# Pooled attention and a gated feed-forward on one core: query loads moved to later slots of a hand-written plan

## The chip, the core and the metric

The kernel runs on one core of a Trainium2 chip. The metric is the device time in microseconds (us) of one execution. TensorE (PE, with its weight loads PEld), VectorE (DVE), ScalarE (ACT) and GpSimd (POOL) work side by side, each in its own program order, and wait for each other by semaphores. SyncE (SP) issues all DMAs here, in its program order too; an issue that has to wait holds up all issues behind it.

## The reference

```python
# q, k, v: (8, 8, 576, 64)  (batch, head, token, dim), float32; pool = 8, so 72 pooled keys
k_p = k.reshape(B, H, 72, 8, 64).mean(axis=3)
v_p = v.reshape(B, H, 72, 8, 64).mean(axis=3)
scores = (1 / sqrt(64)) * q @ k_p.T
attn = softmax(scores)                     # with 1e-09 added to the sum
x = (attn @ v_p) -> (4608 tokens, 512)     # token-major, heads side by side
out = ((x @ w1) * (x @ w2)) @ w3 @ w_out   # w1, w2: 512x1024; w3: 1024x1024; w_out: 1024x512
```

## The kernel before

The product w3 @ w_out is computed once, at the start, into `W`; after that, chunk by chunk of 384 tokens (12 chunks, `NCH`), `a = x @ w1`, `b = x @ w2`, their product g and `out = g @ W`. Float32 factors are split in a high and a low part (fp32r), and each product is done in three passes (high-high, high-low, low-high).

The order of the work is written out by hand. Each step is entered with `at(kind, k, step, ...)` in a plan at a time k, and the plan is then sorted by the whole slot k // 1, the kind ("L" for loads, "P" for the work of VectorE, ScalarE and GpSimd, "M" for the large products, "A" for the products of attention), the fraction of k, and the order of entry. The steps are emitted in that order, so a slot is no time on the chip; it sets the order in which each engine finds its instructions. In a slot, steps of the same fraction stand in the order in which they were entered: first the feed-forward, then attention with its query steps, then keys and values.

A chunk m has 24 slots, three for each of 8 column blocks j:

- slot 3j: `a_mm` (12 matmuls into the PSUM bank `a`), then at 3j + 1 `a_post` (ScalarE, L573) copies it out;
- slot 3j + 1: `b_mm` (12 matmuls, L563, into the bank `b`); at 3j + 2 `b_post` multiplies it on VectorE (L583), which empties the bank, and ScalarE casts the high part gh (L584); at 3j + 2.5 `g_lo` makes the low part gl on VectorE (L589);
- slot 3j + 5: `out_mm` (9 matmuls, L598) with gh and gl. The banks `a` and `b` have one buffer each.

In the slots of chunk m, the attention of chunk n = m + 1 is worked out. A chunk's 384 tokens lie in one batch (three tiles of 128 tokens) or, for n = 1, 4, 7, 10, in two (four tiles of 96). For tile t, counted from the first slot of chunk m:

- scores `s_mm` (TensorE, L404) at slots -1 + 3t and 3t, `soft1`, `soft2`, `soft3` (the softmax on VectorE and ScalarE; `soft3` also gathers the remainder columns R, L451 and L453);
- `pt_turn` at 4 + 3t: VectorE transposes 32x32 blocks of the probabilities and of R into the tile T, which has one buffer (L487, twice);
- `pt_move` at 5 + 3t: SyncE issues a DMA for every 32 tokens (four or three) that move the blocks of T into PTx (L503);
- `pt_split` at 7.5 + 3t: ScalarE casts the high part PTh (L152), VectorE subtracts for the low part (L153);
- `av_mm` (TensorE, L537 to L540) from slot 16 (three tiles) or 18 (four tiles), and `av_post`, which makes the next x.

The queries come in with `load_q`, one call for each of four head pairs, as 32-element rows (4 DMAs a call for a chunk in one batch, 8 for one in two batches; L265), and `tr_q` turns them on VectorE (L276). For chunk n >= 2 the loads stand 18 to 15 slots ahead of the first slot k of chunk n - 1, so at slots 6, 7, 8, 9 of chunk n - 2, and the turns at slots 15 to 18 of it. The buffers `qs` and `qT` have one copy each.

Keys and values of a batch: `load_k` in slots 8, 10, 12, 14 of the chunk before, `prep_k` on GpSimd (a tree of three additions, L362 to L364). For batches from 2 on, `load_v` stands at slots 1 and 2 of the chunk in whose slots the batch is first attended to, `load_vr` (the remainder values: 8 DMAs, L356) at 3, `prep_v` (GpSimd) at 6 and 7, `prep_v2` (a ScalarE cast, L374, then GpSimd, L375) at 9 and 10, `prep_vr` (the GpSimd tree, then three ScalarE operations, L381 to L384) at 10, and `prep_vr2` (GpSimd, L392) at 11. Such chunks are m = 2, 3, 5, 6, 8, 9. The staging tiles `st` of keys, values and remainder values share four buffers in turn.

The outputs of chunk m - 1 are copied out and stored in slot 3 (`out_post`, L610 to L613).

Of the kernel before, what the change touches and what calls it, by code (L numbers as in the profile page):

```python
# [18 lines left out]
def kernel(  # L19
# [228 lines left out]
    def tok_tiles(n):  # L248
        res = []
        for (b, s0, cnt, off) in pieces(n):  # L250
            step = 128 if cnt == 384 else 96
            for x in range(0, cnt, step):
                res.append((b, off + x, step))
        return res
# [382 lines left out]
    def at(kind, k, fn, *args):  # L637


        plan.append((k // 1, "LPMA".index(kind), k % 1, len(plan), fn, args))  # L640

    def plan_att(n, s_at, ds, pt_at, av_at):


        for t in range(len(tok_tiles(n))):
            for half in range(2):
                k = s_at[t] + ds * half
                at("A", k, s_mm, n, t, half)
                at("P", k + 1, soft1, n, t, half)
            at("P", k + 2, soft2, n, t)  # L650
            at("P", k + 3, soft3, n, t)
            if n > 1:
                at("P", k + 4, pt_turn, n, t)
                at("L", k + 5, pt_move, n, t)
                at("P", pt_at[t], pt_split, n, t)
                continue
            k = pt_at[t]
            at("A", k, pt_mm, n, t)
            at("A", k, ptr_mm, n, t)
            at("P", k + 1, pt_post, n, t)  # L660
            at("P", k + 1, ptr_post, n, t)
        for pr in range(NPR):
            at("A", av_at[pr], av_mm, n, pr)
            at("P", av_at[pr] + 1, av_post, n, pr)

    def plan_k(b, k, load, prep, d):
        for pr in range(NPR):
            at("L", load + 2 * pr, load_k, b, pr)
            at("P", prep + d * pr, prep_k, b, pr)
        at("A", k, kt_mm, b)  # L670
        at("P", k + 1, kt_post, b)

    def plan_v(b, load, load_r, prep, prep2, prep_r):
        for hf in range(2):
            at("L", load + hf, load_v, b, hf)
            at("P", prep + hf, prep_v, b, hf)
            at("P", prep2 + hf, prep_v2, b, hf)
        at("L", load_r, load_vr, b)
        at("P", prep_r, prep_vr, b)
        at("P", prep_r + 1, prep_vr2, b)  # L680

    def plan_q(n, load, d_load, turn, d_turn):
        for pr in range(NPR):
            at("L", load + d_load * pr, load_q, n, (pr,))
            at("P", turn + d_turn * pr, tr_q, n, pr)

    def plan_q3(n, load, turn):
        for pr in range(NPR):
            at("L", load[pr], load_q3, n, pr)
            at("A", turn[pr], q3_turn, n, pr)  # L690
            at("P", turn[pr] // 1 + 1.2, q3_post, n, pr)
# [10 lines left out]
    for s in range(NS):  # L702
        k = F0 + 2 * s
# [19 lines left out]
    for j in range(NJ):  # L723
        for w in range(2):
            i = 2 * j + w
            at("L", K0 + 8.5 + i, load_w12, j, w)
            k = M0 - 6 + 1.25 * i
# [5 lines left out]
    for m in range(NCH):  # L733
        m0 = M0 + 3 * NJ * m
        for j in range(NJ):
            k = m0 + 3 * j
# [9 lines left out]
    for n in range(1, NCH):  # L746
        k = M0 + 3 * NJ * (n - 1)
        nt = len(tok_tiles(n))
        s0, pt, av = (3, 5.5, 20.5) if n == 1 else (-1, 8.5, 18) if nt == 4 else (-1, 8.5, 16)
        s_at = [k + s0 + 3 * t for t in range(nt)]  # L750
        plan_att(n, s_at, 1, [x + pt for x in s_at], [k + av + pr for pr in range(NPR)])
        if n == 1:
            plan_q3(n, [K0 + 8.5 + 1.5 * pr for pr in range(NPR)], [K0 + 12, K0 + 13, K0 + 15, K0 + 15.5])
        else:
            plan_q(n, k - 18, 1, k - 9, 1)
    for b in range(1, B):
        k = M0 + 3 * NJ * (3 * (b // 2) + b % 2 - 1)
        if b == 1:
            plan_k(b, k + 3.5, k - 7, k - 4, 2)
            plan_v(b, k + 5, k + 6.5, k + 7, k + 16, k + 13)  # L760
        else:
            plan_k(b, k - 3, k - 16, k - 13, 2)
            plan_v(b, k + 1, k + 3, k + 6, k + 9, k + 10)

    for _, _, _, _, fn, args in sorted(plan, key=lambda x: x[:4]):
        fn(*args)
# [30 lines left out]
```

## Time and profile before

| | |
|---|---|
| median of 3 runs | 830.6 us (828.93 to 830.96) |
| the profiled execution | 824.39 us |
| its span, first to last instruction | 822.6 us |
| mean granted TensorE clock | 0.979 of full speed |
| busy share: PE, DVE, ACT, POOL | 94%, 57%, 34%, 24% |
| DMA issues: q (L265), PTx blocks (L503), remainder values (L356) | 208, 120, 64 |

A row of the timeline has the start, the duration, the engine, the line, the operation with what it writes and reads, and in brackets how long the engine had been idle before it and what ended that. "SPq" is SyncE's queue: a row there is the stretch in which so many DMAs were issued. The table of stretches gives start and end, the length, the busy time of each engine with its instructions, the granted clock, the share of DMA engines busy and GB/s. In the table of waits stand the total, the number and the longest.

### The profile page before, as it was taken

To read this page: it belongs to the slowest core of one execution; us is meant where nothing else is said; L and a number is where in the kernel's file an instruction comes from. 1 tells how busy PE (TensorE), PEld (TensorE's weight loads), DVE (VectorE), ACT (ScalarE), POOL (GpSimd) and SP (SyncE) were. 2 spreads that over 40 slices of the span, in tenths; PEclk is the share of its full clock that TensorE was granted. 3 is DMA by queue.
4 is the path that set the end of the run, shared out by engine and by line. 5 is a ranking of instruction groups with operands and counts; after the bars stand their busy time and mean duration, and the time that the engine had idled before them with its cause. 6 is when DMAs were issued, how large, how long until landed. Compare 5 with 4: busy or idle time off the path is not lost.

```text
span 822.6 us, 11446 instructions
## 1 busy us (share of the span) xinstructions
PE 769.5 (94%) x4146; PEld 712.4 (87%) x4146; DVE 470.3 (57%) x939; ACT 280.1 (34%) x694; POOL 196.6 (24%) x234
## 2 busy tenths in 40 slices
PE   8889877999998998999998998999998999999997
PEld 7668866999987997999987988999987988999997
DVE  7868899384563474484563565474554565572112
ACT  5577654232332332232332322232332232332211
POOL 2335556007027002007037011007036011000000
PEclk9999999999999999999999998999999998999999
DMA  9998940047146040055146140065146140020101
GB/s 326 280 206 219 268 110 1 1 109 162 39 82 143 34 91 16 5 129 137 40 88 142 40 82 15 14 126 131 47 82 141 39 83 15 27 70 0 39 1 39
DMA packets 123913, 74.43 MB, mean 90 GB/s; under 512 B 75600, under 2 KB 107600, under 8 KB 123856
## 3 DMA queue, kind: packets, MB, share of 16 engines
q1 hardware_dynamic: 123856, 73.69, 37.0%
q8 instruction: 33, 0.54, 0.3%
q14 instruction: 24, 0.20, 0.1%
HBM read 52.43 MB, written 9.44 MB: 75 GB/s over the span
## 4 chain that ended last, share of the span: by engine, by line
PE 64%; DVE 15%; DMA 8%; SPq 4%; ACT 4%; issue 3%; POOL 2%; DVEq 0%; ACTq 0%; POOLq 0%
PE b L563 20%; PE o L598 18%; PE a L563 17%; DVE T L487 2%; PE att L404 2%; SPq L265 2%; DMA st<-in_k_dram 2%; SPq L503 2%; DMA PTx<-T 2%; DMA qs<-in_q_dram 2%; DVE mx L420 1%; DVE E L422 1%; ACT E L425 1%; DMA raw<-in_moe_w_dram 1%; DVE E L442 1%
## 5 line engine op out<-in xcount | busy, mean ns | idle before, releaser
L563 PE MATMUL b<-xT,hl 128*128 128x384 f32 x1152 | 229.7, 349 | 26.6 <-DVE a L583 26.1
L563 PEld LDWEIGHTS b<-xT,hl 128*128 128x128 f32 x1152 | 206.1, 194 | 29.8 <-DVE a L583 28.9
L563 PE MATMUL a<-xT,hl 128*128 128x384 f32 x1152 | 223.4, 342 | 0.0
L563 PEld LDWEIGHTS a<-xT,hl 128*128 128x128 f32 x1152 | 203.9, 190 | 4.5 <-POOL hl L153 0.2
L598 PE MATMUL o<-Wc,gh 128*128 128x512 f32 x576 | 182.8, 399 | 0.0
L362 POOL TENSOR_TENSOR st<-st 72x512 f32<-72x512 f32 (+1 forms) x53 | 72.2, 1362 | 218.9 <-DMA st<-in_k_dram 205.3
L598 PEld LDWEIGHTS o<-Wc,gh 128*128 128x128 f32 x576 | 108.9, 192 | 17.5
L598 PE MATMUL o<-Wc,gl 128*128 128x512 f32 x288 | 114.7, 398 | 0.0
L583 DVE TENSOR_TENSOR a<-b,a 128x384 f32<-128x384 f32 x96 | 53.0, 552 | 103.2 <-PE b L563 103.2
L584 ACT CAST gh<-a 128x384 fp32r<-128x384 f32 x96 | 49.3, 513 | 160.0 <-DVE a L583 160.0
L573 ACT COPY a<-a 128x384 f32<-128x384 f32 x96 | 45.9, 479 | 114.6 <-PE a L563 92.4
L425 ACT ACTIVATE E<-E 128x288 f32<-128x288 f32 (+1 forms) x70 | 31.2, 445 | 123.1 <-DVE E L422 123.1
L589 DVE TENSOR_TENSOR gl<-a,gh 128x384 fp32r<-128x384 f32 x96 | 59.9, 624 | 22.7 <-ACT gh L584 22.3
L598 PEld LDWEIGHTS o<-Wc,gl 128*128 128x128 f32 x288 | 54.8, 190 | 12.9
L375 POOL TENSOR_TENSOR vbd<-vm,vbd 64x256 fp32r<-64x256 f32 x16 | 11.9, 745 | 223.3 <-ACT vbd L374 223.1
L153 DVE TENSOR_TENSOR PTx<-PTx,PTh 128x512 fp32r<-128x512 f32 (+1 forms) x33 | 22.2, 673 | 72.0 <-ACT PTh L152 71.6
L549 DVE TENSOR_TENSOR xT<-att,xT 128x384 fp32r<-128x384 f32 x48 | 26.5, 556 | 60.9 <-ACT xT L548 60.9
L404 PE MATMUL att<-kbd,qT 128*128 128x144 f32 (+1 forms) x320 | 52.2, 286 | 0.5 <-ACT E L430 0.5
L426 DVE TENSOR_REDUCE sm<-E 128x4 f32<-128x288 f32 (+1 forms) x70 | 31.6, 452 | 35.8 <-ACT E L425 35.8
L404 PEld LDWEIGHTS att<-kbd,qT 128*128 128x128 f32 (+1 forms) x320 | 47.3, 178 | 4.7 <-ACT E L430 1.1
L420 DVE TENSOR_REDUCE mx<-att 128x4 f32<-128x288 f32 (+1 forms) x80 | 35.2, 440 | 16.2 <-PE att L404 16.1
L363 POOL TENSOR_TENSOR st<-st 72x256 f32<-72x256 f32 (+1 forms) x53 | 42.5, 802 | 4.2
(91 smaller groups left out, 806.2 us busy)
## 6 DMA issues: line engine op xcount, KB each, us to landing
raw<-in_moe_w_dram SPq DMA_DIRECT2D x32, 512.0 KB
PTx<-T SPq DMA_DIRECT2D x120, 96.0 KB
st<-in_k_dram SPq DMA_DIRECT2D x32, 288.0 KB
out_dram<-ob SPq DMA_DIRECT2D x35, 256.0 KB
st<-in_v_dram SPq DMA_DIRECT2D x32, 256.0 KB
qs<-in_q_dram SPq DMA_DIRECT2D x128, 48.0 KB
raw<-in_moe_w_out_dram SPq DMA_DIRECT2D x8, 512.0 KB
st<-in_v_dram SPq DMA_DIRECT2D x64, 64.0 KB
```

The lines of the kernel that those rows point to most:

```text
L362: nc.gpsimd.tensor_tensor(out=t[:, :, 0:4], in0=t[:, :, 0:4], in1=t[:, :, 4:8], op=ALU.add)
L363: nc.gpsimd.tensor_tensor(out=t[:, :, 0:2], in0=t[:, :, 0:2], in1=t[:, :, 2:4], op=ALU.add)
L404: nc.tensor.matmul(out=ps[:nt, 2 * KP * j:2 * KP * (j + 1)], lhsT=qT[n][:, pr, off:off + nt], rhs=kbd[b % 2][:, pr], start=True, stop=True,)
L420: nc.vector.tensor_reduce(out=mx[:nt, hs], in_=sv, axis=AX.X, op=ALU.min)
L425: nc.scalar.activation(out=E[:nt, hs], in_=E[:nt, hs], func=AF.Exp, scale=-1.0)
L426: nc.vector.reduce_sum(out=sm[:nt, hs], in_=E[:nt, hs], axis=AX.X)
L563: nc.tensor.matmul(out=o, lhsT=w12[j, w][sw][:, kt * P:(kt + 1) * P], rhs=x[sx][:, kt], start=(i == 0), stop=(i == 3 * NK - 1))
L573: nc.scalar.copy(out=a, in_=gt[m, j][:, :CH])
L583: nc.vector.tensor_tensor(out=g, in0=ps[:, :CH], in1=g, op=ALU.mult)
L584: nc.scalar.copy(out=gh, in_=g)
L589: nc.vector.tensor_tensor(out=gl, in0=g, in1=f(gh), op=ALU.subtract)
L598: nc.tensor.matmul(out=oacc[m][t], lhsT=(gh, gl)[sg][:, c], rhs=W[j][sw], start=(j == 0 and i == 0), stop=(j == NJ - 1 and i == 2))
```

## The change

For chunks n >= 2, the four query loads go from 18, 17, 16, 15 slots ahead of chunk n - 1 to 11, 9.5, 8 and 6.5, that is from slots 6 to 9 to slots 13, 14, 16 and 17 of chunk n - 2. Their turns go from 9, 8, 7, 6 slots ahead to 8, 6.5, 5 and 3.5 (slots 16, 17, 19, 20). `pt_split` goes half a slot back, from 7.5 + 3t to 8 + 3t; that is a slot of `b_post`, with the same fraction, and so it stands behind `b_post` and ahead of `soft2` and `g_lo`. The remainder values' loads go from slot 3 to 5, where they stand behind the first tile's `pt_move` and so also behind the stores of slot 3; `prep_vr` goes from 10 to 11, where it stands behind the `b_post` and the `pt_split` of that slot, and `prep_vr2` from 11 to 12. Chunk n = 1 and batch 1 keep their plan, but for the queries of chunk 2, which are loaded and turned in the slots of chunk 0.

```diff
@@ -746,13 +746,13 @@
     for n in range(1, NCH):
         k = M0 + 3 * NJ * (n - 1)
         nt = len(tok_tiles(n))
-        s0, pt, av = (3, 5.5, 20.5) if n == 1 else (-1, 8.5, 18) if nt == 4 else (-1, 8.5, 16)
+        s0, pt, av = (3, 5.5, 20.5) if n == 1 else (-1, 9, 18) if nt == 4 else (-1, 9, 16)
         s_at = [k + s0 + 3 * t for t in range(nt)]
         plan_att(n, s_at, 1, [x + pt for x in s_at], [k + av + pr for pr in range(NPR)])
         if n == 1:
             plan_q3(n, [K0 + 8.5 + 1.5 * pr for pr in range(NPR)], [K0 + 12, K0 + 13, K0 + 15, K0 + 15.5])
         else:
-            plan_q(n, k - 18, 1, k - 9, 1)
+            plan_q(n, k - 11, 1.5, k - 8, 1.5)
     for b in range(1, B):
         k = M0 + 3 * NJ * (3 * (b // 2) + b % 2 - 1)
         if b == 1:
@@ -760,7 +760,7 @@
             plan_v(b, k + 5, k + 6.5, k + 7, k + 16, k + 13)
         else:
             plan_k(b, k - 3, k - 16, k - 13, 2)
-            plan_v(b, k + 1, k + 3, k + 6, k + 9, k + 10)
+            plan_v(b, k + 1, k + 5, k + 6, k + 9, k + 11)
```

## The prediction

> **What bounds the kernel now.** I read the page first, then TensorE's waits, then the busy table cut at the first `a` product of each chunk (chunks 1 to 9, so that a row holds one chunk's `a` and `b` products), and last the timelines of single waits.
>
> ```profile
> span 822.6 us, 11446 instructions
> PE 769.5 (94%) x4146; PEld 712.4 (87%) x4146; DVE 470.3 (57%) x939; ACT 280.1 (34%) x694; POOL 196.6 (24%) x234
> ...
> PE b L563 <- DVE a L583: 26.1, 9, 4.1
> ```
>
> TensorE sets the time, and from chunk 1 on it waits for one thing: nine times, 26.1 us in all, the product `b` (L563) waits until VectorE's `b_post` (L583) has emptied the bank `b`.
>
> ```profile
> 158.94:215.31 56.37, 56.37 (x311) 52.99 (x309) 32.72 (x67) 17.11 (x40) 15.50 (x18) 1.00 0.44 99
> 215.31:278.46 63.15, 58.28 (x312) 54.40 (x310) 32.56 (x67) 18.13 (x44) 21.55 (x27) 0.97 0.39 88
> 278.46:341.92 63.46, 59.69 (x332) 55.92 (x330) 36.87 (x81) 18.92 (x47) 6.98 (x9) 0.97 0.20 44
> 341.92:398.23 56.31, 56.31 (x312) 53.09 (x310) 32.60 (x67) 16.75 (x39) 15.50 (x18) 1.00 0.44 99
> 398.23:461.19 62.96, 58.42 (x311) 54.50 (x310) 31.90 (x67) 18.23 (x44) 21.64 (x27) 0.97 0.39 88
> 461.19:526.03 64.84, 60.79 (x331) 56.97 (x330) 37.04 (x81) 18.92 (x47) 6.98 (x9) 0.95 0.19 44
> 526.03:582.35 56.32, 56.32 (x312) 53.09 (x310) 32.29 (x67) 16.74 (x39) 15.46 (x18) 1.00 0.44 99
> 582.35:645.88 63.53, 58.46 (x311) 54.59 (x310) 33.10 (x67) 18.24 (x44) 21.55 (x27) 0.97 0.38 88
> 645.88:710.40 64.52, 60.76 (x331) 56.94 (x330) 36.98 (x81) 18.91 (x47) 6.55 (x9) 0.95 0.19 43
> ```
>
> Columns: stretch, length, busy us and instructions of PE, PEld, DVE, ACT, POOL, then granted clock, DMA share, GB/s. Chunks 1, 4, 7 have TensorE busy throughout at clock 1.00. Chunks 2, 5, 8 do the same matmuls in 6.78, 6.65 and 7.21 us more; 3, 6, 9 (a four-tile attention, 20 matmuls more) also idle 3.8 to 4.1 us, and their clock is lower. These six chunks are where values are loaded. The waits in chunks 2 and 3:
>
> ```profile
> 246.41 2.35 PE L563 MATMUL b<-xT,hl 128*128 128x384 f32 x12 [1.14 <-DVE a L583]
> 256.69 3.76 PE L563 MATMUL b<-xT,hl 128*128 128x384 f32 x12 [3.73 <-DVE a L583]
> ...
> 302.86 2.37 PE L563 MATMUL b<-xT,hl 128*128 128x384 f32 x12
> ...
> 307.16 2.27 PE L563 MATMUL a<-xT,hl 128*128 128x384 f32 x12
> 313.21 3.27 PE L563 MATMUL b<-xT,hl 128*128 128x384 f32 x12 [3.77 <-DVE a L583]
> ```
>
> The waits of 3.7 us are followed by slow products (3.76 and 3.27 us against 2.27 for an `a`); the wait of 1.14 us isn't (2.35). So a long wait costs more than itself.
>
> **Why `b_post` is late.** VectorE and ScalarE work in program order. `pt_split` (ScalarE L152, then VectorE L153) now stands just ahead of `b_post`, and whatever holds it up holds `b_post` up. The 3.73 us, by SyncE's queue, ScalarE and VectorE:
>
> ```profile
> 229.53 7.86 SPq L265 DMA_DIRECT2D qs<-in_q_dram  x16
> 237.50 2.51 SPq L503 DMA_DIRECT2D PTx<-T  x4
> 240.06 4.00 SPq L265 DMA_DIRECT2D qs<-in_q_dram  x8
> ...
> 250.28 2.50 SPq L503 DMA_DIRECT2D PTx<-T  x4
> 260.29 5.38 SPq L356 DMA_DIRECT2D st<-in_v_dram  x8
> ...
> 233.72 0.61 DVE L487 STREAM_TRANSPOSE T<-R 128x256 f32<-128x256 f32 x1
> 241.98 1.12 DVE L487 STREAM_TRANSPOSE T<-E 128x512 f32<-128x512 f32 x1 [2.79 <-DMA PTx<-T]
> 243.00 0.62 DVE L487 STREAM_TRANSPOSE T<-R 128x256 f32<-128x256 f32 x1
> 254.83 0.62 ACT L152 CAST PTh<-PTx 128x512 fp32r<-128x512 f32 x1 [7.55 <-DMA PTx<-T]
> 255.48 0.69 DVE L153 TENSOR_TENSOR PTx<-PTx,PTh 128x512 fp32r<-128x512 f32 x1 [7.81 <-ACT PTh L152]
> 256.09 0.55 DVE L583 TENSOR_TENSOR a<-b,a 128x384 f32<-128x384 f32 x1
> ```
>
> One q load takes 7.86/16 = 0.49 us of the queue. The second tile's T was ready at 234.33, but 16 q loads kept its move until 237.50; that held the third turn (2.79 us of waiting), done at 243.62, and eight and eight more q loads kept the third move until 250.28. It landed at about 254.8, and `b_post` ran at 256.09. The 3.77 us has another cause:
>
> ```profile
> 243.62 0.30 ACT L381 CAST vrh<-vrm 128x128 fp32r<-128x128 f32 x1 [3.59 <-POOL vrm L364]
> 256.67 0.51 ACT L584 CAST gh<-a 128x384 fp32r<-128x384 f32 x1 [1.23 <-DVE a L583]
> ...
> 306.73 0.45 DVE L426 TENSOR_REDUCE sm<-E 96x4 f32<-96x288 f32 x1 [0.51 <-ACT E L425]
> 310.67 0.30 ACT L381 CAST vrh<-vrm 128x128 fp32r<-128x128 f32 x1 [3.54 <-POOL vrm L364]
> 311.60 0.49 ACT L152 CAST PTh<-PTx 128x384 fp32r<-128x384 f32 x1
> 312.13 0.56 DVE L153 TENSOR_TENSOR PTx<-PTx,PTh 128x384 fp32r<-128x384 f32 x1 [4.95 <-ACT PTh L152]
> ```
>
> Here `prep_vr` (L381) stands ahead of `pt_split` on ScalarE, and waits 3.54 us for GpSimd's tree. The 1.14 us in chunk 2 is the same wait (3.59 us, until 243.62) ahead of the second tile's split.
>
> **The change part by part.** No instruction is added or removed.
>
> *`pt` 8.5 to 9.* The split goes from slot 7 (+.5) to slot 8, behind `b_post` and ahead of `soft2` and `g_lo`. In the four-tile chunk `b_post` for product 3 no longer waits for the splitter; its product ended near 302.86 + 2.37 = 305.2 and VectorE was free near 306.73 + 0.45 = 307.2. Cost: after `b_post`, ScalarE must cast gh (0.51) and PTh (0.49 to 0.62) before VectorE can subtract, so VectorE idles about 1.1 us in each of 33 places, and `soft2`, `g_lo` and the next turn come 1.1 us later. The cover for that is below, under the second and the last rival.
>
> *Remainder values: loads 3 to 5, `prep_vr` 10 to 11.* On ScalarE `prep_vr` now follows gh and the split, so its 3.5 us wait holds only the next `soft3` and `a_post`. The eight loads (5.38 us of queue) go behind the first tile's move, which ended at 229.53, so they are out at 234.9; before, with the q loads there, the second move began at 237.50, now at 234.9, 2.6 us earlier. The data must arrive by about 241, when GpSimd's tree began in chunk 2 (its result held ScalarE to 243.6). In a queue that is free the loads are out 6 us ahead of that.
>
> *Queries: slots +13, 14.5, 16, 17.5 of the chunk before.* All q loads of a three-tile chunk now follow the last move, and of a four-tile chunk only one quarter (4 loads, 2 us) stands ahead of it, while that move still waits for its turn. So the second move goes at 234.9 and the third near 242.5 (its turn, no longer waiting, ends there), 8 us earlier; it lands before the split in slot 14. The q loads, at most 32 x 0.49 = 15.7 us with the k loads among them, run from 245 to 261. Their turns are now at slots 16 to 20.5. With chunk 2 at 56.4 us from 215.31, these slots lie at 253 to 264 and the chunk ends near 272, where the scores need the last of them; the four quarters are issued by 249, 253, 257 and 261. VectorE may reach the first turn at 249 and wait 2 us for its data, ahead of a `b_post` whose product isn't done before 253. Cost 0, cover 2 to 7 us; if a quarter came later than that, `b_post` would wait as before.
>
> *Chunk 0.* Query turns also move here:
>
> ```profile
> 137.62 0.56 DVE L276 STREAM_TRANSPOSE qT<-qs 128x384 f32<-128x384 f32 x1
> ...
> 138.55 2.08 DVE L453 TENSOR_TENSOR R<-E,R 96x64 fp32r<-96x64 f32 x2
> ...
> 140.78 0.55 PE L474 MATMUL att<-ident,R 96*128 96x96 f32 x2 [2.42 <-DVE R L453]
> ```
>
> The first turn leaves its place ahead of R. That is 0.56 us at once; if the two R subtractions, 2.08 us here, also escape what stretched them, all of the 2.42 us go, and with them what a slow product behind costs (1.0 to 1.5 us behind the two long waits above): 3.9 at most. In the other direction this crowded stage could lose as much. I take 2, nearer to the upper end, since R's inputs are then ready before that stretch.
>
> **The sum.** Chunks 2, 5, 8 come down to the length of 1, 4, 7: 6.78 + 6.65 + 7.21 = 20.6. Chunks 3, 6, 9 lose idle and slow clock: (63.46 - 59.69) + 0.03 x 59.69 = 5.6; 4.05 + 0.05 x 60.79 = 7.1; 3.76 + 0.05 x 60.76 = 6.8; 19.5 in all. Chunk 0: 2. Less 1 for new short waits in the four-tile chunks, which become tight (first rival). 41.1 us. The profiled execution took 824.39 us (its span 822.6), so 783.3; the median of the runs shown is 830.6, 0.8% above it, and 830.6 x 783.3/824.39 = 789.
>
> **The rivals.**
>
> *The four-tile chunks trade their wait for another (0.14): 797.* Adding the 1.1 us, `b_post` 3 ends near 308.7 and TensorE wants its bank at 307.16 + 2.1 = 309.25: 0.5 us to spare. Then `prep_vr` delays `soft3`, so the fourth turn ends near 315.1, `b_post` 4 near 315.6, and the bank is wanted at 315.55. GpSimd's tree now runs beside VectorE's subtractions instead of in its idle time, and one such had to pay:
>
> ```profile
> 263.04 1.48 DVE L589 TENSOR_TENSOR gl<-a,gh 128x384 fp32r<-128x384 f32 x1
> ```
>
> 0.9 us longer beside GpSimd; three such operations in the slot give 2.7 us per chunk, three chunks 8: 789 + 8 = 797. The Trainium skill ("SBUF — State Buffer", Who interferes with whom) says that a VectorE instruction with two SBUF inputs contends with a GpSimd instruction that reads SBUF; both inputs of L589 are in SBUF, and by that rule this rival comes about each time and the time is 797; the trace agrees with it in the row above (1.48 us beside the tree, against 0.55 us for the `g_lo` shown below), but doesn't show how often the two will meet.
>
> *The remainder loads hold the second move instead of the q loads (0.06): 810.* If their data were still moving when the second move is issued, its blocks would land late, the third turn wait, and `b_post` in chunks 2, 5, 8 with it: those keep their 20.6 us. Against it: 5.4 us of queue stand where 7.9 stood.
>
> *The waits stay (0.04): about 830.* If `b_post` were late by VectorE's own load, not by the splits, order wouldn't matter. The 7.81 and 4.95 us of idle VectorE in front of L153 speak against it.
>
> *Slower (0.04): 845.* `g_lo`, now behind the split's wait, becomes what TensorE waits for. In chunk 2:
>
> ```profile
> 238.36 0.55 DVE L589 TENSOR_TENSOR gl<-a,gh 128x384 fp32r<-128x384 f32 x1
> ...
> 241.37 0.39 PE L598 MATMUL o<-Wc,gl 128*128 128x512 f32 x1
> ```
>
> It ended at 238.91, will end near 240.15, and is wanted at 241.37: 1.2 us to spare. Each us beyond costs 33 us over the 33 places; the gain of 41 is gone when `g_lo` comes 1.2 + 41/33 = 2.5 us later than I work out, and at half a us more the time is 830.6 + 16 = 847, say 845.
>
> **How the numbers follow.** My forecast (all nine waits gone, at most short ones new) has 0.72: 789, by itself 783 to 794. The lower end is the profiled execution's level with nothing new lost. To leave out no more than two in ten the range takes in the rival at 797 and goes some way to 810: 783 to 806. Runs of one kernel here spread over 0.25%, so 0.3% is about what can be told from no change. Faster: 0.72 + 0.14 + 0.06 = 0.92. Same: 0.03 and slower 0.05, from the last two rivals and what of "waits stay" falls to either side.
>
> **What would show it.** Right: no wait of `b` for L583 over 1.2 us; chunks 2, 5, 8 at 56 to 57 us and 3, 6, 9 at 57 to 59, all at clock 1.00; the third move of chunk 2 issued within 1 us of its turn; ScalarE's wait at L381 still there in chunk 3, but behind L152; `qT` turns with little wait. Wrong: a new row of `b` or `o` behind L583 or L589 in the four-tile chunks (first rival), a wait of the T turn for the PTx move of 2 us or more (second), `o` behind L589 in all chunks (last).

## The result, and the profile after

The changed kernel takes 789.5 us (median of 4 runs, 787.77 to 790.49) against 830.3 us: a ratio of 0.951 (95% interval 0.949 to 0.953), 40.8 us less. The forecast was 789. Of all the runs below only one fell in a slow state (1243.6 us at a granted clock of 0.56, a run of the kernel with issues but no data), and it stands in none of the figures. The profiled execution took 787.77 us, 36.6 less than the profiled one of before; its span by chunks, cut as before at each chunk's first `a` product (length, busy us and instructions of PE, PEld, DVE, ACT, POOL, granted clock, DMA share, GB/s):

```profile
158.64:215.00 56.36, 56.36 (x311) 52.97 (x309) 33.90 (x67) 16.95 (x40) 16.14 (x18) 1.00 0.41 89
215.00:271.31 56.31, 56.31 (x312) 53.06 (x310) 32.59 (x67) 18.16 (x44) 22.23 (x27) 1.00 0.41 99
271.31:330.44 59.13, 58.09 (x332) 54.43 (x330) 38.05 (x81) 18.84 (x47) 6.06 (x10) 1.00 0.24 56
330.44:386.76 56.32, 56.32 (x311) 53.10 (x310) 33.98 (x67) 16.57 (x39) 15.98 (x18) 1.00 0.40 90
386.76:443.07 56.31, 56.31 (x311) 53.07 (x310) 33.72 (x67) 18.16 (x44) 21.28 (x26) 1.00 0.40 99
443.07:502.20 59.13, 58.09 (x331) 54.45 (x330) 38.05 (x81) 18.84 (x47) 6.76 (x11) 1.00 0.24 57
502.20:558.53 56.33, 56.33 (x312) 53.11 (x310) 32.72 (x67) 16.57 (x39) 16.51 (x18) 1.00 0.41 89
558.53:614.84 56.31, 56.31 (x311) 53.06 (x310) 32.84 (x67) 18.16 (x44) 21.34 (x26) 1.00 0.41 99
614.84:673.97 59.13, 58.09 (x332) 54.44 (x330) 38.05 (x81) 18.84 (x47) 6.96 (x11) 1.00 0.24 56
```

All nine chunks run at clock 1.00 now. Chunks 2, 5, 8 are as long as 1, 4, 7. The four-tile chunks 3, 6, 9 keep 59.13 - 58.09 = 1.04 us of idle TensorE each. No wait of `b` for L583 is left; the page and TensorE's waits show what is:

```profile
span 785.9 us, 11514 instructions
PE 759.7 (97%) x4146; PEld 703.7 (90%) x4146; DVE 479.2 (61%) x939; ACT 278.5 (35%) x694; POOL 201.1 (26%) x234
...
PE o L598 <- DVE gl L589: 3.1, 3, 1.0
```

SyncE's queue in chunk 2, where the first tile's move, the remainder loads, the second and third moves and the query loads now follow each other:

```profile
226.63 2.54 SPq L503 DMA_DIRECT2D PTx<-T  x4
229.27 5.42 SPq L356 DMA_DIRECT2D st<-in_v_dram  x8
234.79 2.54 SPq L503 DMA_DIRECT2D PTx<-T  x4
...
241.52 2.50 SPq L503 DMA_DIRECT2D PTx<-T  x4
244.12 0.50 SPq L307 DMA_DIRECT2D st<-in_k_dram  x1
244.66 4.00 SPq L265 DMA_DIRECT2D qs<-in_q_dram  x8
...
249.16 11.50 SPq L265 DMA_DIRECT2D qs<-in_q_dram  x24
```

The third move goes at 241.52 (250.28 before) and the query loads run from 244.66 to 260.66.

Nearly all of the 36.6 us of the profiled pair lies here: chunks 2, 5, 8 give 6.84 + 6.65 + 7.22 = 20.7 (against 56.31); 3, 6, 9 give 4.33 + 5.71 + 5.39 = 15.4 (against 59.13); chunk 0 gives 3.7; and the part ahead of it took 3.4 more, which the change doesn't touch:

```profile
0.00:83.39 83.39, 72.63 (x390) 60.62 (x391) 65.53 (x119) 54.10 (x138) 31.52 (x44) 1.00 0.96 259
83.39:158.94 75.55, 63.38 (x355) 58.29 (x353) 58.72 (x95) 38.03 (x109) 33.36 (x29) 0.95 0.41 98
```

(before), and after:

```profile
0.00:86.80 86.80, 77.41 (x390) 64.12 (x391) 67.30 (x118) 53.72 (x138) 35.76 (x45) 0.94 0.96 259
86.80:158.64 71.84, 61.98 (x354) 56.93 (x353) 58.02 (x96) 37.87 (x109) 32.05 (x27) 0.98 0.41 91
```

In the 14 profiles of this study that first part took 83.4 to 90.4 us, with its DMA engines busy (share 0.93 to 0.98), and the profiled execution before had the shortest. That may be why the profiled pair shows less than the medians; the other runs have no profile that could show it.

### The profile page after: what moved, and what is told of

Its sections match the earlier page's. It is cut to its first block, busy times and chain, and to the rows that moved or that the text cites. A ratio compares the mean times of both kernels' runs of the same rounds, so it can differ in the third digit from the quotient of the medians.

```text
span 785.9 us, 11514 instructions
## 1 busy us (share of the span) xinstructions
PE 759.7 (97%) x4146; PEld 703.7 (90%) x4146; DVE 479.2 (61%) x939; ACT 278.5 (35%) x694; POOL 201.1 (26%) x234
## 4 chain that ended last, share of the span: by engine, by line
PE 74%; DVE 15%; ACT 3%; DMA 3%; issue 3%; SPq 1%; DVEq 0%
PE o L598 22%; PE a L563 21%; PE b L563 21%; PE att L404 3%; DMA st<-in_v_dram 2%; PE o L624 2%; DVE T L487 2%; DVE E L442 1%; DVE wb L148 1%; DVE wb L140 1%; PE att L538 1%; PE att L540 1%; PE att L539 1%; DVE mx L420 1%; PE att L537 1%
## 5 line engine op out<-in xcount | busy, mean ns | idle before, releaser
L563 PE MATMUL b<-xT,hl 128*128 128x384 f32 x1152 | 220.8, 339 | 0.4 <-DVE Wc L153 0.4
L563 PEld LDWEIGHTS b<-xT,hl 128*128 128x128 f32 x1152 | 199.7, 188 | 0.8 <-DVE Wc L153 0.8
L598 PE MATMUL o<-Wc,gh 128*128 128x512 f32 x576 | 180.6, 395 | 0.0
L362 POOL TENSOR_TENSOR st<-st 72x512 f32<-72x512 f32 (+1 forms) x53 | 77.8, 1469 | 224.5 <-DMA st<-in_k_dram 172.1
L598 PEld LDWEIGHTS o<-Wc,gh 128*128 128x128 f32 x576 | 106.7, 188 | 17.0
L583 DVE TENSOR_TENSOR a<-b,a 128x384 f32<-128x384 f32 x96 | 52.8, 550 | 112.6 <-PE b L563 112.6
L589 DVE TENSOR_TENSOR gl<-a,gh 128x384 fp32r<-128x384 f32 x96 | 64.0, 667 | 13.0 <-ACT gh L584 13.0
L153 DVE TENSOR_TENSOR PTx<-PTx,PTh 128x512 fp32r<-128x512 f32 (+1 forms) x33 | 24.7, 749 | 35.1 <-ACT PTh L152 31.7
L363 POOL TENSOR_TENSOR st<-st 72x256 f32<-72x256 f32 (+1 forms) x53 | 44.4, 837 | 4.2
```

The source lines that it names most:

```text
L362: nc.gpsimd.tensor_tensor(out=t[:, :, 0:4], in0=t[:, :, 0:4], in1=t[:, :, 4:8], op=ALU.add)
L363: nc.gpsimd.tensor_tensor(out=t[:, :, 0:2], in0=t[:, :, 0:2], in1=t[:, :, 2:4], op=ALU.add)
L563: nc.tensor.matmul(out=o, lhsT=w12[j, w][sw][:, kt * P:(kt + 1) * P], rhs=x[sx][:, kt], start=(i == 0), stop=(i == 3 * NK - 1))
L583: nc.vector.tensor_tensor(out=g, in0=ps[:, :CH], in1=g, op=ALU.mult)
L589: nc.vector.tensor_tensor(out=gl, in0=g, in1=f(gh), op=ALU.subtract)
L598: nc.tensor.matmul(out=oacc[m][t], lhsT=(gh, gl)[sg][:, c], rhs=W[j][sw], start=(j == 0 and i == 0), stop=(j == NJ - 1 and i == 2))
```

## The experiments

The theory: three things made `b_post` late, each removed by a part of the change. Query loads held the second and third moves on SyncE's queue; `prep_vr` held the second split on ScalarE until GpSimd's tree was done; and the split stood ahead of `b_post`, so that both reached it. The rival for each part: it alone did it, or it did nothing. "Split" is the half slot, "queries" the query loads and turns, "values" the remainder loads and `prep_vr`. Ratios are to the kernel before on the same chip.

| split | queries | values | median us | ratio (95% interval) | TensorE's waits from chunk 1 on |
|---|---|---|---|---|---|
| - | - | - | 827.4 to 830.3 | 1 | `b` for L583 26.1 |
| x | - | - | 817.4 | 0.987 (0.983 to 0.991) | `o` and attention 17.4 |
| - | x | - | 806.3 | 0.973 (0.970 to 0.976) | `b` for L583 15.0 |
| - | - | x | 835.2 | 1.009 (1.006 to 1.012) | `b` for L583 30.1 |
| - | x | x | 786.2 | 0.949 (0.946 to 0.952) | none |
| x | - | x | 818.1 | 0.987 (0.984 to 0.991) | `b` 14.7, `o` and attention 6.1 |
| x | x | - | 807.3 | 0.975 (0.971 to 0.978) | `o` 13.0 |
| x | x | x | 789.5; 789.1 | 0.951; 0.953 (0.950 to 0.956) | `o` for L589 3.1 |

**The split alone.**

```diff
-... (-1, 8.5, 18) if nt == 4 else (-1, 8.5, 16)
+... (-1, 9, 18) if nt == 4 else (-1, 9, 16)
```

> Of the change only the split's half slot (pt 9) on the kernel before. My theory (each of the three parts takes away one cause, the wait comes back elsewhere if a cause stays): no wait of b for L583 is left, but the causes stay, so TensorE waits on other rows: about 2.7 us a chunk in chunks 2, 5, 8 (attention's product L537 or out, behind the third split whose blocks land late) and 3.3 us in chunks 3, 6, 9 (out L598 for gh or gl, held by prep_vr's wait on ScalarE). Time about 815 us (805 to 822). Rival (the order alone did it, the other two parts are decoration): 788 to 795 us.

Measured 817.4. TensorE's waits from chunk 1 on:

```profile
PE o L598 <- DVE gl L589: 7.4, 5, 2.3
PE o L598 <- ACT gh L584: 5.3, 3, 2.0
PE att L537 <- ACT PTh L152: 3.5, 3, 1.7
```

No `b` waits, but `o` waits for gh and gl, and attention for the split: the delay is passed to the next reader. In chunks 2, 5, 8 that is 1.5 to 2.3 us of waits, less than the 2.7 expected, and 3.9 to 4.2 in 3, 6, 9, more than the 3.3 expected. Yet chunks 5 and 8 are 60.49 and 60.81 us long, over 4 more than the 56.31 of a chunk without a wait, since slow products follow there (chunk 5; the `o` pairs of 1.05 us take 0.62 otherwise):

```profile
436.47 0.44 PE L537 MATMUL att<-PTh,vbd 128*128 128x384 f32 x1 [0.91 <-ACT PTh L152]
437.51 0.45 PE L538 MATMUL att<-PTx,vbd 128*128 128x384 f32 x1 [0.60 <-DMA st<-in_k_dram]
...
438.14 1.05 PE L598 MATMUL o<-Wc,gh 128*128 128x512 f32 x2
```

The rival, that the order alone did it, falls: the order alone brings 1.3%.

**The queries alone.**

```diff
-            plan_q(n, k - 18, 1, k - 9, 1)
+            plan_q(n, k - 11, 1.5, k - 8, 1.5)
```

> Of the change only the queries' loads and turns. My theory: the 3.7 us waits of chunks 2, 5, 8 go, with their slow products (about 5.5 us each); the waits of 1.1 us there and of 3.8 us in chunks 3, 6, 9 stay, because prep_vr still stands ahead of the second split on ScalarE. Time about 813 us (808 to 818). Rival (late query loads are what delayed everything): all nine waits go, 788 to 795 us.

Measured 806.3, just under my range. Of the nine waits exactly the three of the third move are gone; in this profile 1.15, 1.13, 1.13 and 3.78, 4.05, 3.78 us stay. Chunks 2, 5, 8 gave 16.4 us, as expected. What the range missed is that chunk 0 gave 3.4 and chunks 6 and 9 gave 1.1 each, and that the kernel before took 827.8 us on this chip, not 830.3.

**The values alone.**

```diff
-            plan_v(b, k + 1, k + 3, k + 6, k + 9, k + 10)
+            plan_v(b, k + 1, k + 5, k + 6, k + 9, k + 11)
```

> Of the change only the remainder values (loads at slot 5, prep_vr at 11). My theory: the 3.8 us waits of chunks 3, 6, 9 go; but the eight loads now stand with the query loads between the first and the second tile's move, so the second move goes out near 243 instead of 237.5 in chunk 2's time, and chunks 2, 5, 8 wait some 8 us instead of 4.9. Time about 822 us (812 to 832). Rival (each part helps by itself, the parts add up): 806 to 812 us.

Measured 835.2, above my range and 0.9% over the kernel before. SyncE's queue in chunk 2:

```profile
226.44 2.59 SPq L503 DMA_DIRECT2D PTx<-T  x4
229.13 5.42 SPq L356 DMA_DIRECT2D st<-in_v_dram  x8
234.59 7.80 SPq L265 DMA_DIRECT2D qs<-in_q_dram  x16
242.50 2.54 SPq L503 DMA_DIRECT2D PTx<-T  x4
```

The remainder loads add their 5.4 us to the query loads' 7.8 and the second move goes at 242.50; `b` waits 5.1 to 5.3 us once and 1.8 to 3.7 us a second time in each of chunks 2, 5, 8. The waits of chunks 3, 6, 9, which I expected to go, only fell to 1.7, 2.3 and 2.7 us: there too the remainder loads and eight query loads now stand ahead of the second move, and in chunk 3 the next T turn waits 2.19 us for it. The parts don't add up: this one costs 7 us alone and, on top of the queries (806.3 to 786.2), saves 20.

**Issues without their data.** Added to the changed kernel:

```diff
             plan_q(n, k - 11, 1.5, k - 8, 1.5)
+            for pr in range(NPR):
+                at("L", k - 18 + pr, tiny, n, pr)
```

`tiny` issues 4 or 8 DMAs, as many as the `load_q` call in whose old slot it stands.

> The changed kernel, and in the old slots 6 to 9 as many DMAs as there were query loads, each of 512 bytes (32 rows of 16) into a scratch tile that nothing reads: SyncE's issues come back without their data. My theory (a move is late because of the time that issues before it take on SyncE's queue, 0.4 to 0.5 us each): the second and third moves of chunks 2, 5, 8 are late again and waits of some us come back there; about 812 us (803 to 824). Rival (the 128-byte packets of the queries crowd the DMA engines): no wait comes back, 788 to 792 us.

```profile
225.08 2.54 SPq L515 DMA_DIRECT2D PTx<-T  x4
227.72 5.42 SPq L368 DMA_DIRECT2D st<-in_v_dram  x8
233.19 7.46 SPq L278 DMA_DIRECT2D scr<-in_q_dram  x16
240.75 2.56 SPq L515 DMA_DIRECT2D PTx<-T  x4
```

Measured 813.9 (median of three), ratio 0.981 (0.977 to 0.986). Sixteen 512-byte DMAs take 7.46 us of the queue, 0.47 each, against 0.49 for the 24 KB of a query load. `b` waits 3.8 to 4.2 us in chunks 2, 5, 8 again, and these chunks take 63.0 to 63.8 us; with the query loads themselves in the old slots (the change without the queries, below) they take 63.4 to 64.8. So it is the issue far more than the data that made the moves late.

**The change without its split**, the two parts above together.

> The changed kernel with the split back in its old slot (pt 8.5). My theory: with the moves early and prep_vr behind, the split finds its data and no ScalarE wait ahead of it, so it doesn't hold up b_post; all long waits stay away. The three waits of out for gl go, since g_lo isn't behind the split; b_post of chunks 3, 6, 9 is close (0.5 us) and may wait up to 1.1 us for VectorE's subtraction beside GpSimd. Time 786 to 792 us. Rival (the order of split and b_post is what counts): 800 us or more.

Measured 786.2: no wait at all from chunk 1 on, and chunks 3, 6, 9 at 58.2 us. With the moves early and `prep_vr` behind, the split's half slot isn't needed; it costs the three `o` waits.

**The change without the queries**: their loads and turns as in the kernel before.

> The changed kernel with the queries' loads and turns back in their old slots. My theory: the remainder loads and the query loads together hold the second move by 5 us or more, the T turn waits for it, and b waits for L583 behind it in chunks 2, 5, 8: 5 to 8 us of waiting a chunk; chunks 3, 6, 9 stay short. Time about 818 us (808 to 830). Rival (with the split behind b_post late moves are harmless): 788 to 795 us.

Measured 818.1. `b` waits 4.1 to 4.7 us in chunks 2, 5, 8: with the split behind `b_post`, the T turn, which stands ahead of `b_post`, still waits for the late move (7.65 us in chunk 2).

**The change without the values**: remainder loads and `prep_vr` as in the kernel before.

> The changed kernel with the remainder loads and prep_vr back at slots 3 and 10. My theory: chunks 2, 5, 8 stay at 56 to 57 us, but in chunks 3, 6, 9 prep_vr holds gh and the split on ScalarE for 3.5 us, and out waits about 3.3 us for gh and gl, more than the 1.0 us that it waits now, with some slow clock. Time about 800 us (795 to 805). Rival (prep_vr's place doesn't matter once the split is behind b_post): 788 to 792 us.

Measured 807.3, a little over my range. Chunk 3:

```profile
305.32 0.73 PE L598 MATMUL o<-Wc,gh 128*128 128x512 f32 x2 [1.67 <-ACT gh L584]
308.31 0.79 PE L598 MATMUL o<-Wc,gl 128*128 128x512 f32 x1 [2.25 <-DVE gl L589]
308.90 1.05 PE L598 MATMUL o<-Wc,gh 128*128 128x512 f32 x2
```

3.9 us of waiting in two pieces, and then slow products (1.05 us for two matmuls that take 0.62): the chunk is 65.0 us long, 5.9 over the changed kernel's.

**The tree in GpSimd's idle time**, on the kernel before. `prep_vr` keeps ScalarE's part.

```diff
+    def vr_tree(b):
+        m = stage["vrt", b] = p1.tile([P, 2, D], F32, tag="vrm", name="vrm")
+        pool_tree(stage.pop(("vr", b)), m)
...
+            at("P", k + 7.5, vr_tree, b)
```

> The kernel before, with only GpSimd's tree of the remainder values taken out of prep_vr and put at slot 7.5, ahead of prep_v2, in GpSimd's idle time; ScalarE's part stays at slot 10. My theory (the waits of 1.1 us and of 3.8 us in chunks 3, 6, 9 come from ScalarE waiting for this tree): ScalarE's 21.4 us of waiting at L381 go, and with them those waits; the 3.7 us waits of chunks 2, 5, 8 stay. Time about 808 us (803 to 813). Rival (the waits come from VectorE's load and the split's place): 825 us or more.

Measured 811.1. The waits at L381 are gone from ScalarE's list, and with them the three of 3.8 us and the three of 1.1 us, but for four short ones (0.24 to 0.53); chunks 3, 6, 9 are 58.4 to 58.6 us long. The third move's waits stay, and grow to 4.4 to 5.1 us, since TensorE comes there sooner. This shows GpSimd's tree as the cause of those six.

**The last microsecond.** In the changed kernel's chunk 3, VectorE, then GpSimd, then the wait of TensorE:

```profile
300.97 0.55 DVE L583 TENSOR_TENSOR a<-b,a 128x384 f32<-128x384 f32 x1
302.51 1.08 DVE L153 TENSOR_TENSOR PTx<-PTx,PTh 128x384 fp32r<-128x384 f32 x1 [0.99 <-ACT PTh L152]
303.52 0.70 DVE L439 TENSOR_SCALAR sm<-sm 96x8 f32<-96x8 f32 x1
...
305.27 0.54 DVE L589 TENSOR_TENSOR gl<-a,gh 128x384 fp32r<-128x384 f32 x1
...
301.89 1.29 POOL L362 TENSOR_TENSOR st<-st 128x512 f32<-128x512 f32 x1
303.25 0.94 POOL L363 TENSOR_TENSOR st<-st 128x256 f32<-128x256 f32 x1
...
305.87 0.50 PE L598 MATMUL o<-Wc,gl 128*128 128x512 f32 x1 [1.04 <-DVE gl L589]
```

L153 takes 1.08 instead of 0.56 and ends 0.4 us after GpSimd's L362 (303.18); L439 takes 0.70 instead of 0.16 and ends as L363 does (304.19). The Trainium skill ("SBUF — State Buffer", Who interferes with whom) says that a VectorE instruction with two SBUF inputs contends with a GpSimd instruction that reads SBUF, that a tensor_scalar can too, in a two-port mode, and that the order of issue decides which of the two is blocked; these rows agree, since L362 began before L153 and L363 before L439. With the 0.99 us in which VectorE idles for the casts that makes two candidates for the 1.04 us that TensorE waits for gl. Three kernels went at this, with the changed kernel again on the same chip:

> The changed kernel again, beside the next three on one chip: 787 to 791 us, and three waits of out for gl of 1.0 us in chunks 3, 6, 9.

Measured 789.1, with the three waits.

```diff
-... (-1, 9, 18) if nt == 4 else (-1, 9, 16)
+... (-1, 9.75, 18) if nt == 4 else (-1, 9, 16)
-            plan_v(b, k + 1, k + 5, k + 6, k + 9, k + 11)
+            plan_v(b, k + 1, k + 5, k + 6, k + 9, k + (11.8 if b % 2 else 11))
```

> The changed kernel, with the split of four-tile chunks a further 0.75 slot back, behind soft2 and g_lo (pt 9.75), and prep_vr of their batch behind it (11.8). My theory (the 1.04 us waits of out come from g_lo standing behind the split, whose subtraction and whose soft2 are stretched beside GpSimd's tree): g_lo ends a us sooner and the three waits go, chunks 3, 6, 9 at 57.6 to 58.2 us instead of 59.1: 786 us against the changed kernel's 789 (2 to 4 us less). Rival (b_post is late by itself there): unchanged or a new wait of b.

Measured 785.3, ratio 0.949 (0.946 to 0.952); no wait of TensorE from chunk 1 on, chunks 3, 6, 9 at 57.9 to 58.0 us in the profile. `g_lo` ahead of the split is enough, though the contention is still there (L442 took 1.69 instead of 0.76).

The changed kernel with `vr_tree` at 7.5:

> The changed kernel, with GpSimd's tree of the remainder values at slot 7.5, ahead of prep_v2, so that it runs some 8 us earlier and not beside slot 11; the split stays ahead of g_lo. Theory A (contention of VectorE with the tree makes the 1.04 us wait): L153 and L439 of slot 11 come back to 0.56 and 0.16 us, the three waits go; but slot 8 gets the contention, with 1.2 us to spare in chunks 2, 5, 8 (short waits possible). Time 785 to 789 us. Theory B (the wait is VectorE's 1.0 us of idling for the casts): waits of 0.5 us or more stay in chunks 3, 6, 9, 788 to 790 us.

Measured 790.5: neither theory's number. The six runs fall in two groups, 788.4 to 788.6 and 792.3 to 793.3 us, and the profile is one of the second. Its chunk 3, slots 8 and 11:

```profile
297.88 1.64 DVE L597 TENSOR_TENSOR gl<-a,gh 128x384 fp32r<-128x384 f32 x1
...
306.92 0.56 DVE L153 TENSOR_TENSOR PTx<-PTx,PTh 128x384 fp32r<-128x384 f32 x1 [0.99 <-ACT PTh L152]
307.39 0.16 DVE L447 TENSOR_SCALAR sm<-sm 96x8 f32<-96x8 f32 x1
...
297.32 1.78 POOL L362 TENSOR_TENSOR st<-st 128x512 f32<-128x512 f32 x1 [20.80 <-DMA PTx<-T]
```

Slot 11 is clean, as theory A has it, but the tree met `g_lo` of slot 8 (1.64 instead of 0.55). That delay ran on through VectorE's work to `b_post` (0.4 to 0.9 us of waiting) and `g_lo` (0.55) of slot 11. The contention was moved, not removed, so this run doesn't separate its share from that of the casts.

The tree at 7.5 and no split:

> The changed kernel with both: the split in its old slot (pt 8.5) and the tree at 7.5. Neither ScalarE's wait at L381 nor the split's wait for casts is left ahead of b_post or g_lo: all chunks from 1 to 9 at their least, 56.3 and 57.6 us. Time 784 to 787 us, 3 to 4 less than the changed kernel's; against the changed kernel with only the split put back (786.2 measured) 0 to 2 us less.

Measured 786.6, in the expected range, but with two `b` waits of 0.6 us left (chunks 3 and 9), which I had not expected. The three versions at 785.3, 786.2 and 786.6 can't be told from each other; `g_lo` first has the lowest median, and its profile is without a wait.

## Why the prediction was right

*The cause of the nine waits*: right, and shown part by part. All nine are gone with the three parts, the three of 3.7 us go with the queries alone, and the other six, down to four short ones of at most 0.53 us, with the tree's wait alone.

*The split*: its place behind `b_post` was taken for one of the things that bring the gain. That step failed: without it the kernel is as fast or faster (786.2). It brings something only where moves are late: ratio 1.009 to 0.987 beside the values, 0.973 to 0.975 beside the queries. What I costed as 1.1 us of idle VectorE measures 0.99 and 1.10.

*The values*: the second move was put at 234.9 and went at 234.79. The remainder loads fit in the queue because the query loads had left it; alone they are a loss, which the prediction did not say.

*The queries*: third move forecast near 242.5, measured 241.52; loads forecast from 245 to 261, measured 244.66 to 260.66. VectorE took the first turn at 250.33 with no wait for its data, where I allowed 2 us.

*The sum*: chunks 2, 5, 8 forecast 20.6, measured 20.7. Chunks 3, 6, 9 forecast 19.5 less 1, measured 15.4: the short waits were under-sized. A four-tile chunk without a wait takes 57.94 us (`g_lo` first), so what remains in the changed kernel costs 59.13 - 57.94 = 1.2 us a chunk, not a third of one. Chunk 0 forecast 2, measured 3.7: the R subtractions did escape what stretched them, and the wait before the R transpose fell from 2.42 to 0.21 us:

```profile
141.38 0.34 DVE L453 TENSOR_TENSOR R<-E,R 96x64 fp32r<-96x64 f32 x2
141.86 0.35 PE L474 MATMUL att<-ident,R 96*128 96x96 f32 x2 [0.21 <-DVE R L453]
```

The kernels with the queries' part have chunk 0 at 71.8 to 72.3 us, those without at 74.0 to 75.8. Together the chunks gave 39.8 us where I had 41.1: 3.1 too much in chunks 3, 6, 9 against 1.7 too little in chunk 0. That 789 is met within a us is luck: the misses offset each other, the profiled pair differs by 36.6 us and the medians by 40.8, and no trace shows where the medians' extra 4 us lie.

*The rivals*: the first came about in small, in its place (slot 11 of the four-tile chunks, `o` behind L589), at less than half its price (3 x 1.2 = 3.6 us of 8). In slot 11 two VectorE operations were stretched beside GpSimd by 0.52 and 0.54 us and a third by 0.1, where three times 0.9 had been allowed; the row of 1.48 us behind the 0.9 stood beside the tree of the values, not of the remainder values. The stretching is there, but how much of the wait is due to it, and how much to the casts, stays open. `b_post` 3 and the fourth turn of chunk 3 ended 30.2 and 36.8 us into the chunk, as worked out under this rival (30.2 and 36.6). The second didn't come: the second move left on time. Nor did the last: `g_lo` of chunk 2 was not waited for.

## What to carry to other kernels

When an engine in program order is late, ask for each instruction ahead of it what it waits for; moving the late one ahead of the waiting one hands most of the wait to the next reader (17.4 us of 26.1 stay, 817.4 us), while with the causes removed the old order is as good or better (786.2). On a queue of small DMAs like this one count issues, not bytes: a transfer that others wait for belongs ahead of loads that have time. Parts of a change can be worth less than nothing alone and much together, so test them by leaving each out as well as by putting each in.

## What the runs showed of the hardware

A 512-byte DMA holds SyncE's queue for 0.47 us, a 24 KB one of 192 short rows for 0.49. In the chunks 1 to 9 of all profiles here the granted clock, where it drops, reads 0.50 for 3.4 us or twice that: in the kernel before from 256.4 to 259.8 us, at the end of the 3.73 us wait. That is why a long wait costs more than itself: this chunk is 63.15 - 56.31 = 6.84 us longer than one without a wait, and its waits are 4.87. A single wait of TensorE of 1.0 to 1.2 us was followed by no slow product (the changed kernel's 59.13 us chunks hold one, at clock 1.00), nor was one of 1.69 us (the values alone, chunk 3), but one of 2.27 us was (chunk 6 there). Two waits of 0.91 and 0.60 us with one product between them were, and so were 1.67 and 2.25 us, but 0.93 and 0.28 us (the split alone, chunk 2) were not. Why is open. The Trainium skill ("TensorE: Matmul & The Clock Gate", HAM oscillation) puts the slow clock behind idle gaps of over about 3.4 us; these runs differ, since it came behind waits much shorter than that, single ones and pairs. A VectorE operation of 0.16 us took 0.70 beside GpSimd's additions, though it reads a 96x8 tile.
